# HGRN2 attention into a rational-Padé layer on one core: 1/Q written over its own denominator, four buffers for h, p1 and p2 in whole units, and a rewritten order

## The chip, the core and the metric

The kernel runs on one core of a Trainium2 chip. The core has four engines that compute, each working through its own list of instructions in order: TensorE (PE in the profile, with its weight loads as PEld), VectorE (DVE), ScalarE (ACT) and GpSimd (POOL). SyncE (SP) issues loads and stores; GpSimd issues those that convert a type or add into their destination. All transfers share 16 DMA engines. An engine waits for another by semaphores, and everything behind a waiting instruction on its engine waits too.

The metric is device microseconds (us) for the whole program, lower is better. The kernel before was measured at 213.81, 214.25 and 214.86 us (median 214.25).

## The reference

```python
# attention: B=4, H=8, S=768, D=48
f = 1.0 / (1.0 + np.exp(-f_logit))
for t in range(S):
    state = f[:, :, t, :, None] * state + np.einsum('bhd,bhe->bhde', k[:, :, t], v[:, :, t])
    y[:, :, t] = np.einsum('bhd,bhde->bhe', q[:, :, t], state)
x = y.transpose(0, 2, 1, 3).reshape(B * S, H * D)          # 3072 x 384
# rational layer: w_in 384 x 2048, w_out 2048 x 384
h = x @ w_in
P = a[0] + a[1] * h + a[2] * h**2 + a[3] * h**3
Q = 1.0 + abs(b[0]) * abs(h) + abs(b[1]) * h**2
out = (P / (Q + 1e-06)) @ w_out
```

## The kernel before

The 3072 tokens are cut into 12 **units** of 256 tokens of one batch (unit n is chunk n // 4 of batch n % 4). A unit passes through attention and then through the rational layer. The layer's 2048 features are 16 column blocks of 128; a step on blocks 0 to 8 or 8 to 16 works on one half of the unit (128 x 2048 numbers in bf16), a step on 0 to 16 on both at once (128 x 4096).

The work is not scheduled by a compiler. The string `ORDER` (lines 19 to 99) is a hand-kept list of about 800 steps, and each engine executes its instructions in the order in which the list records them. A step is written `name unit arguments`. `@k` gives the step one of four PSUM slots, which it gets when the last reader of the slot's earlier contents is done. `!mK` names an instruction, and `^mK` on another makes that one wait until the named one is done (`behind`, line 578); this is how GpSimd's work is held back. The steps, with the engine that runs them:

- `ld` loads f, k, q (SP) or v (GpSimd, with a cast to bf16); `wi` and `wo` load w_in and w_out (GpSimd, with a cast), in eight and four pieces.
- Attention: `ef`, `ls` (ACT) make log(1 + exp(-f)); `cs` (PE) sums it over tokens; `A` (ACT) takes exp of the sums; `xa n x` (line 330) multiplies q (x = 0) or k (x = 1) by it, whole (128 x 768) or in halves (128 x 384), on DVE, or on GpSimd where the step ends in `p`; `T` (PE) transposes, `Te` copies it out of PSUM; `sc`, `mk` are the masked scores (PE, DVE); `ic`, `si`, `st` advance the state (PE, PE, DVE); `vm` copies columns of v; `yi`, `yb` (PE) and `ye` (ACT or DVE) make x.
- Rational layer: `h` (PE, line 472) multiplies by w_in, four blocks into one slot; `hy` (ACT, line 487) copies them to SBUF as bf16. `sq` (DVE) or `sa` (ACT) squares into h2; `ab` (DVE) writes |h| into z; `zv` (DVE) or `zd` (an adding DMA that GpSimd issues) adds h2 to z; `rq` (ACT, line 513) takes 1/Q of z. `p1` (DVE, line 524) writes a3 h + a2 into g; `pm` (DVE) multiplies g by h2; `p2` (DVE, line 529) writes a1 h + a0 over h; `tv` (DVE) or `ta` (adding DMA) adds that to g; `gm` (DVE, line 546) multiplies g by 1/Q. `o` (PE, line 550) multiplies by w_out, `oe` copies out and `so` stores.

The arrays of the layer live in rings of buffers: unit n uses buffer n mod the ring's size (line 172):

```python
for key, n in (("hy", 3), ("h2", 2), ("z", 2), ("g", 3), ("qi", 2)):
    rings(key, n, [KF, NT], BF16)
```

So `hy` of unit n may begin once the last reader of h of unit n - 3 (its `ta` or `tv`) is done, `ab` of unit n once `rq` of unit n - 2 is, `rq` of unit n once `gm` of unit n - 2 is, and `p1` of unit n once `o` of unit n - 3 is.

ScalarE needs one table for exp and log and another for 1/Q; `tab` switches them.

Of the kernel before, what the change touches and what calls it, by code (L numbers as in the profile page):

```python
# [8 lines left out]
F32 = mybir.dt.float32  # L9
# [15 lines left out]
xa 1 0 0 2; Te 0 2 4 s; xa 1 0 2 4; ef 2; si 0 1; sc 0 1 @0; xa 1 1 0 2; st 0 1; T 1 @1; mk 0 0; ld 2 k
mk 0 1 !m5; yb 0 0 2 @3; yi 0 1; Te 1; ef 3; yb 0 2 4; ic 1 @2; ls 2; st 1 0 !m1; sc 1 1 @0; ld 2 v ^m1
ye 0 s; cs 2 @1; mk 1 1 !m3; ls 3; sc 1 0 @3; wi 0 0 8; A 2 0; si 1 1; ld 5 f; cs 3 @0; wi 3 0 8; st 1 1
A 2 1; vm 1 v !m4; wi 2 0 8; mk 1 0; xa 2 0 0 2 p ^m0; A 3 0; h 0 8 12 @2; wi 1 0 8; xa 2 0 2 4; h 0 12 16 @1
hy 0 8 12; cz 4; fb; ld 4 f; yb 1 0 2 @3; hy 0 12 16; yb 1 2 4; xa 2 1; yi 1 1; ye 1 s; p1 0 8 16; T 2 @2
# [12 lines left out]
st 5 0; yb 4 0 2; tv 0 0 8 !m8; si 5 1; hy 2 0 4; h 3 4 8 @0; ld 6 q; ld 6 v ^m8; st 5 1; gm 0 0 8; yi 4 1
# [65 lines left out]
def kernel(  # L108
# [63 lines left out]
    for key, n in (("hy", 3), ("h2", 2), ("z", 2), ("g", 3), ("qi", 2)):  # L172
        rings(key, n, [KF, NT], BF16)
# [71 lines left out]
    def const_z(i):  # L245
# [383 lines left out]
```

## Time and profile before

| | us |
|---|---|
| median of three runs | 214.25 |
| the profiled execution: its time | 213.87 |
| its span from first to last instruction | 212.2 |
| PE busy in it | 190.1 |
| DVE busy in it | 190.8 |
| ACT busy in it | 186.7 |
| POOL busy in it | 81.5 |

The profile is of one execution. The clock that TensorE was granted was 0.994 of full speed over the span. A row of a group of instructions reads: line, engine, operation, out<-in, shapes, xcount, then busy time, mean ns of one and the idle time of the engine before them. A row of a timeline reads: start, duration, engine, line, operation, and in brackets the idle time before it with what ended it. Instructions of one engine that follow each other without a wait overlap a little in these records (the next one starts before the one ahead is recorded as ended), so the time from start to start is somewhat shorter than the duration.

### The profile page before, as it was taken

The numbers are of one execution on the slowest core, as the hardware profiler recorded it, in microseconds if no ns is written. First come the engines' busy times: TensorE is split into PE (matmuls) and PEld (weight loads), VectorE is DVE, ScalarE is ACT, GpSimd is POOL, SyncE is SP. The second block draws the span as 40 slices with busy tenths as digits, with TensorE's granted clock in tenths as the row PEclk, the third lists the DMA queues.
The fourth block names the chain that finished last, engine by engine and source line by source line (L and its number), as shares of the span: only waits on it lengthen the run. The fifth ranks groups of instructions, "written<-read, shape, count | busy, mean of one in ns | idle before, by whom it ended". The sixth has DMA issues, their size and how long they took to land.

```text
span 212.2 us, 6607 instructions
## 1 busy us (share of the span) xinstructions
PE 190.1 (90%) x2894; PEld 138.7 (65%) x2894; DVE 190.8 (90%) x236; ACT 186.7 (88%) x172; POOL 81.5 (38%) x99
## 2 busy tenths in 40 slices
PE   1296799997789999999999899999999999999991
PEld 1165587875568678766888567678766766775650
DVE  3269689999999999999999979999999999999970
ACT  4755689999887999999999699999999999999861
POOL 6050612329943438016351750551583433402000
PEclk9999999999999999999999999999999999999997
DMA  5999998999999189999999999799899999998955
GB/s 93 276 251 208 249 223 229 246 259 199 180 204 209 37 153 153 228 283 279 206 232 253 245 199 219 163 195 205 171 195 162 211 206 195 198 197 167 235 152 170
DMA packets 61820, 43.15 MB, mean 203 GB/s; under 512 B 51424, under 2 KB 56544, under 8 KB 61792
## 3 DMA queue, kind: packets, MB, share of 16 engines
q0 software_dynamic: 20528, 23.86, 68.4%
q1 hardware_dynamic: 41184, 18.78, 34.2%
q8 instruction: 22, 0.36, 0.6%
q10 hardware_dynamic: 80, 0.10, 0.2%
q14 instruction: 6, 0.05, 0.1%
HBM read 25.17 MB, written 4.72 MB: 141 GB/s over the span
## 4 chain that ended last, share of the span: by engine, by line
PE 60%; DVE 15%; DMA 12%; ACT 5%; issue 3%; POOL 3%; SPq 2%; POOLq 0%; ACTq 0%; DVEq 0%
PE op L557 28%; PE hp L477 19%; DMA w_in_sb<-in_moe_w_in_dram 5%; PE y L391 4%; DMA g<-hy 4%; DVE scm L378 3%; DMA k<-in_k_dram 3%; PE tp L347 3%; DVE qkp L333 2%; DVE g L536 2%; PE sc L370 2%; PE cs L306 2%; DVE h L493 2%; ACT qi L516 2%; DVE state L461 1%
## 5 line engine op out<-in xcount | busy, mean ns | idle before, releaser
L477 PE MATMUL hp<-x,w_in_sb 128*128 128x256 bf16 x576 | 68.0, 273 | 1.1 <-DVE state L461 0.9
L557 PE MATMUL op<-w_out_sb,g 128*128 128x384 bf16 x384 | 68.6, 326 | 0.0
L477 PEld LDWEIGHTS <-w_in_sb 128*128 128x128 bf16 x576 | 55.5, 98 | 10.4 <-issue 1.9
L489 ACT CAST hy<-hp 128x1024 bf16<-128x1024 f32 x48 | 47.8, 1027 | 5.0 <-PE hp L477 3.1
L557 PEld LDWEIGHTS <-g 128*128 128x128 bf16 x384 | 35.8, 98 | 23.8 <-issue 1.2
L516 ACT ACTIVATE qi<-z 128x4096 bf16<-128x4096 bf16 (+1 forms) x16 | 44.4, 2777 | 1.1 <-DVE z L507 1.1
L511 POOL DMA_DIRECT2D z<-h x20 | 21.5, 1120 | 26.1 <-ACT h L498 18.1
L378 DVE TENSOR_TENSOR scm<-sc,mask 128x1024 bf16<-128x1024 f32 x24 | 28.8, 1214 | 1.5 <-PE sc L370 1.4
L548 DVE TENSOR_TENSOR g<-g,qi 128x2048 bf16<-128x2048 bf16 (+2 forms) x24 | 28.9, 1217 | 0.9 <-ACT qi L516 0.7
L536 DVE TENSOR_TENSOR g<-g,h 128x2048 bf16<-128x2048 bf16 (+1 forms) x21 | 29.4, 1401 | 0.1
L498 ACT ACTIVATE h<-hy 128x2048 bf16<-128x2048 bf16 (+1 forms) x13 | 26.8, 2072 | 0.0
L540 POOL DMA_DIRECT2D g<-hy x15 | 13.8, 938 | 28.1 <-DVE g L536 10.4
L328 ACT ACTIVATE A<-cs 128x768 f32<-128x768 f32 (+3 forms) x26 | 19.0, 779 | 4.5 <-PE cs L314 4.5
L333 POOL TENSOR_TENSOR qkp<-k,A 128x384 bf16<-128x384 f32 x11 | 13.0, 1218 | 23.4 <-DVE g L548 10.6
L306 PE MATMUL cs<-lsp,Ui 128*128 128x384 bf16 (+1 forms) x39 | 11.1, 345 | 10.4 <-ACT lsp L296 10.4
L526 DVE TENSOR_SCALAR g<-hy,a_sb 128x2048 bf16<-128x2048 bf16 (+1 forms) x23 | 19.0, 832 | 0.6 <-ACT hy L489 0.6
L209 POOL DMA_DIRECT2D v<-in_v_dram x12 | 12.4, 1037 | 17.6 <-DVE state L461 8.8
L531 DVE TENSOR_SCALAR hy<-hy,a_sb 128x2048 bf16<-128x2048 bf16 (+1 forms) x20 | 18.6, 928 | 0.4
L333 POOL TENSOR_TENSOR qkp<-q,A 128x384 bf16<-128x384 f32 x10 | 12.6, 1268 | 9.9 <-ACT A L328 5.3
L502 DVE TENSOR_SCALAR z<-hy 128x2048 uint16<-128x2048 uint16 (+1 forms) x21 | 15.7, 759 | 0.0
L347 PE MATMUL tp<-ident,qkp 128*128 128x128 bf16 x192 | 13.7, 227 | 2.0 <-DVE qkp L333 1.4
L391 PE MATMUL y<-scm,v 64*32 64x128 bf16 x384 | 14.0, 218 | 0.8 <-DVE scm L378 0.7
(71 smaller groups left out, 245.0 us busy)
## 6 DMA issues: line engine op xcount, KB each, us to landing
z<-h POOLq DMA_DIRECT2D x20, 512.0 KB, 7.2
g<-hy POOLq DMA_DIRECT2D x15, 512.0 KB, 7.5
f<-in_f_logit_dram SPq DMA_DIRECT2D x11, 384.0 KB, 6.9
k<-in_k_dram SPq DMA_DIRECT2D x11, 384.0 KB, 8.2
q<-in_q_dram SPq DMA_DIRECT2D x11, 384.0 KB, 7.5
v<-in_v_dram POOLq DMA_DIRECT2D x12, 192.0 KB, 7.3
out_dram<-f SPq DMA_DIRECT2D x12, 192.0 KB, 3.6
out_dram<-osb SPq DMA_DIRECT2D x10, 192.0 KB, 5.0
```

The lines of the kernel that those rows point to most:

```text
L333: i = (nc.gpsimd if eng == "p" else nc.vector).tensor_mul(s["qk"][:, x, :, hh, 0:D], s["qk"[x]][:, hh].rearrange("p h i d -> p i h d"), s[ ...
L347: nc.tensor.transpose(t[:, x, i, p, :], s["qk"][:, x, i, 2 * p:2 * p + 2, :].rearrange("t h d -> t (h d)"), ident)
L378: return nc.vector.tensor_mul(t, s["sc", g].rearrange("s r a i t -> s (r a) (i t)"), mb)
L391: nc.tensor.matmul(s["y"][32 * a:32 * a + 32, j, kk * C:kk * C + C].rearrange("e (i t) -> e i t", i=2), lhsT, rhs, start=(j, a) not in s[" ...
L477: nc.tensor.matmul(t[:, m - m0, :].rearrange("f (j t) -> f j t", j=UB), w_in_sb[:, kk, m * P:(m + 1) * P], s["x"][:, :, kk, :], start=(kk ...
L489: nc.scalar.copy(fl(big(s, "hy"), m0, m1), fl(s["hp", m0], 0, m1 - m0))
L498: return nc.scalar.activation(fl(big(s, "h2"), m0, m1), fl(big(s, "hy"), m0, m1), AF.Square)
L511: return nc.gpsimd.dma_start(out=fl(big(s, "z"), m0, m1), in_=fl(big(s, "h2"), m0, m1), accum_op=ALU.add)
L516: return nc.scalar.add_instruction(mybir.InstActivation(name=nc.get_next_instruction_name(), func=AF.Reciprocal, ins=[nc.scalar.lower_ap(f ...
L536: return nc.vector.tensor_mul(fl(big(s, "g"), m0, m1), fl(big(s, "g"), m0, m1), fl(big(s, "h2"), m0, m1))
L548: return nc.vector.tensor_mul(fl(big(s, "g"), m0, m1), fl(big(s, "g"), m0, m1), fl(big(s, "qi"), m0, m1))
L557: nc.tensor.matmul(s["op", g][:, j, 0:DM], big(s, "g")[:, m, C * j:C * j + C], w_out_sb[:, m, :], start=(s["on", j] == 1), stop=(s["on", j ...
```

## The change

The ring `qi` is gone, and `rq` writes 1/Q over z, from where `gm` reads it. z has three buffers in place of two, and hy four in place of three, so that the space stays what it was. A step that nothing used (`dm`) and the memset of its zeros (`cz 4`) are gone. The list of steps is rewritten throughout; two of its lines stand here for all.

```diff
-cu 1; cz 1; ld 0 f 2 4; ld 0 v; ab_ b s; cz 3; cz 0; ld 0 f 0 2; ci; ld 0 q 2 4; ld 1 f; cu 0; ld 0 k 0 2
-ef 0 2 4; ls 0 2 4; cm; ld 0 k 2 4; cz 2; fa; cs 0 2 4 @0; ef 0 0 2; ls 0 0 2; ld 0 q 0 2; cs 0 0 2 @1; ld 1 k
+ci; ld 0 f 0 2; cu 1; ld 0 f 2 4; ld 0 q 0 2; ld 0 v; ab_ b s; ld 1 f; cu 0; ld 0 k 0 2; ef 0 0 2; ls 0 0 2
+cm; ef 0 2 4; cz 1; ld 0 k 2 4; ls 0 2 4; cz 0; ld 0 q 2 4; cz 2; cz 3; cs 0 2 4 @0; cs 0 0 2 @1; ld 1 q
...
-    for key, n in (("hy", 3), ("h2", 2), ("z", 2), ("g", 3), ("qi", 2)):
+    for key, n in (("hy", 4), ("h2", 2), ("z", 3), ("g", 3)):
         rings(key, n, [KF, NT], BF16)
...
-        elif i == 4:
-            return nc.vector.memset(zz, 0.0)
...
             outs=[nc.scalar.lower_ap(fl(big(s, "qi"), m0, m1))]))
+            outs=[nc.scalar.lower_ap(fl(big(s, "z"), m0, m1))]))
...
-        return nc.vector.tensor_mul(fl(big(s, "g"), m0, m1), fl(big(s, "g"), m0, m1), fl(big(s, "qi"), m0, m1))
+        return nc.vector.tensor_mul(fl(big(s, "g"), m0, m1), fl(big(s, "g"), m0, m1), fl(big(s, "z"), m0, m1))
```

Counted over the two lists, the steps whose number or width differs are these:

| step | before | after |
|---|---|---|
| p1 on both halves / on one | 1 / 22 | 5 / 14 |
| p2 on both halves / on one | 4 / 16 | 5 / 14 |
| ab on both halves / on one | 3 / 18 | 0 / 24 |
| rq on both halves / on one | 8 / 8 | 6 / 12 |
| xa on DVE, whole / in halves | 4 / 19 | 2 / 24 |
| xa on GpSimd | 21 | 20 |
| Te on DVE, oe on DVE | 1, 0 | 2, 1 |

The xa that leaves GpSimd is that of q of unit 2, heads 0 to 3. Te of the first half of unit 0 goes from ACT to DVE, as does one of the last two oe.

Three places of the lists follow, engine by engine. A number right behind a name is the buffer of the ring (hy1 is buffer 1 of hy), the number behind the underscore is the build's own.

**First place: ScalarE around the copies of h of unit 7.** Before, unit 7 is in hy1 (and unit 6 in hy0), and 1/Q of unit 3 is written to qi1:

```order
L516 ACTIVATE qi1_117<-z1_112 128x2048
L454 ACTIVATE x3_137<-y_2227 128x768
L489 CAST hy0_106<-hp_2213 128x1024
L489 CAST hy0_106<-hp_2321 128x1024
L489 CAST hy0_106<-hp_2197 128x1024
L516 ACTIVATE qi1_117<-z1_112 128x2048
L489 CAST hy1_107<-hp_2354 128x1024
L357 COPY T0_132<-tp_2371 128x1024
L489 CAST hy1_107<-hp_2339 128x1024
L516 ACTIVATE qi0_116<-z0_111 128x4096
```

After, unit 7 is in hy3:

```order
L508 ACTIVATE z0_111<-z0_111 128x2048
L452 ACTIVATE x3_136<-y_2193 128x768
L481 CAST hy2_107<-hp_2241 128x1024
L481 CAST hy2_107<-hp_2319 128x1024
L481 CAST hy3_108<-hp_2335 128x1024
L508 ACTIVATE z0_111<-z0_111 128x2048
L355 COPY T0_131<-tp_2350 128x1024
L481 CAST hy2_107<-hp_2302 128x1024
L481 CAST hy3_108<-hp_2370 128x1024
L508 ACTIVATE z1_112<-z1_112 128x4096
```

One copy of unit 7 has moved ahead of the second 1/Q, the other behind Te of unit 8; hy1 was last used by unit 4, hy3 by unit 3.

**Second place: GpSimd and VectorE around the loads of w_out.** The COPY is vm, the TENSOR_TENSOR are xa. GpSimd before:

```order
L333 TENSOR_TENSOR qkp0_80<-q1_125,A0_130 128x2x4x48
L511 DMA z0_111<-h20_109 128x2048
L333 TENSOR_TENSOR qkp0_80<-k1_122,A0_130 128x2x4x48
L385 COPY vmp1_85<-v0_127 128x8x2x16
L209 DMA v2_129<-in_v_dram 128x8x96
L221 DMA w_out_sb_105<-in_moe_w_out_dram 128x4x384 x3
L333 TENSOR_TENSOR qkp1_81<-k2_123,A1_131 128x2x4x48 x2
L385 COPY vmp0_84<-v1_128 128x8x2x16
L221 DMA w_out_sb_105<-in_moe_w_out_dram 128x4x384
L333 TENSOR_TENSOR qkp1_81<-q2_126,A1_131 128x2x4x48 x2
```

GpSimd after:

```order
L331 TENSOR_TENSOR qkp0_79<-q1_124,A0_129 128x2x4x48
L503 DMA z0_111<-h20_109 128x2048
L383 COPY vmp1_84<-v0_126 128x8x2x16
L331 TENSOR_TENSOR qkp0_79<-k1_121,A0_129 128x2x4x48
L209 DMA v2_128<-in_v_dram 128x8x96
L221 DMA w_out_sb_104<-in_moe_w_out_dram 128x4x384 x2
L331 TENSOR_TENSOR qkp1_80<-k2_122,A1_130 128x2x4x48 x2
L383 COPY vmp0_83<-v1_127 128x8x2x16
L221 DMA w_out_sb_104<-in_moe_w_out_dram 128x4x384
L331 TENSOR_TENSOR qkp1_80<-q2_125,A1_130 128x2x4x48 x2
L221 DMA w_out_sb_104<-in_moe_w_out_dram 128x4x384
```

VectorE in the same stretch, before:

```order
L378 TENSOR_TENSOR scm0_133<-sc_944,mask_76 128x1024
L461 TENSOR_TENSOR state3_1_96<-sv_981,A1_131 128x384
L493 TENSOR_TENSOR h20_109<-hy0_106 128x2048
L536 TENSOR_TENSOR g0_113<-g0_113,h20_109 128x2048
L461 TENSOR_TENSOR state3_2_97<-sv_981,A1_131 128x384
L378 TENSOR_TENSOR scm0_133<-sc_1035,mask_76 128x1024
L333 TENSOR_TENSOR qkp0_80<-k1_122,A0_130 128x2x4x48
L333 TENSOR_TENSOR qkp0_80<-q1_125,A0_130 128x2x4x48
L526 TENSOR_SCALAR g1_114<-hy1_107,a_sb_98 128x2048
L536 TENSOR_TENSOR g1_114<-g1_114,h21_110 128x2048
```

and after:

```order
L376 TENSOR_TENSOR scm0_132<-sc_959,mask_76 128x1024
L331 TENSOR_TENSOR qkp0_79<-q1_124,A0_129 128x2x4x48
L485 TENSOR_TENSOR h20_109<-hy0_105 128x2048
L528 TENSOR_TENSOR g0_114<-g0_114,h20_109 128x2048
L459 TENSOR_TENSOR state3_2_96<-sv_941,A1_130 128x384
L376 TENSOR_TENSOR scm0_132<-sc_1031,mask_76 128x1024
L331 TENSOR_TENSOR qkp0_79<-k1_121,A0_129 128x2x4x48
L518 TENSOR_SCALAR g1_115<-hy1_106,a_sb_97 128x2048
L528 TENSOR_TENSOR g1_115<-g1_115,h21_110 128x2048
```

VectorE's q product of unit 4 has moved ahead of the square of unit 0, the other stays behind the scores of unit 3; one of GpSimd's four loads of w_out has moved behind its products of unit 5.

**Third place: VectorE from gm of unit 1 to p1 of unit 4.** Before, p1 of units 3 and 4 (L526) are half steps:

```order
L548 TENSOR_TENSOR g1_114<-g1_114,qi1_117 128x2048 x2
L502 TENSOR_SCALAR z1_112<-hy0_106 128x2048 x2
L493 TENSOR_TENSOR h20_109<-hy1_107 128x2048
L526 TENSOR_SCALAR g0_113<-hy0_106,a_sb_98 128x2048
L548 TENSOR_TENSOR g2_115<-g2_115,qi0_116 128x2048
L536 TENSOR_TENSOR g0_113<-g0_113,h21_110 128x2048
L548 TENSOR_TENSOR g2_115<-g2_115,qi0_116 128x2048
L378 TENSOR_TENSOR scm0_133<-sc_1873,mask_76 128x1024
L378 TENSOR_TENSOR scm0_133<-sc_1855,mask_76 128x1024
L526 TENSOR_SCALAR g1_114<-hy1_107,a_sb_98 128x2048
```

After:

```order
L540 TENSOR_TENSOR g1_115<-g1_115,z1_112 128x2048 x2
L485 TENSOR_TENSOR h20_109<-hy0_105 128x2048
L494 TENSOR_SCALAR z1_112<-hy0_105 128x2048
L518 TENSOR_SCALAR g0_114<-hy3_108,a_sb_97 128x4096
L540 TENSOR_TENSOR g2_116<-g2_116,z2_113 128x4096
L518 TENSOR_SCALAR g1_115<-hy0_105,a_sb_97 128x4096
L376 TENSOR_TENSOR scm0_132<-sc_1843,mask_76 128x1024
```

p1 of unit 4 (into g1, which unit 1 used) is one step of 4096 now, and stands ahead of the scores of unit 6 instead of behind them.

More of the change, by code (lines that the diff above doesn't have):

```diff
@@ L25 @@
[L25 to L29, printed above, removed]
@@ L464, in st @@
             _at(s["ae"], [[DM + 16 if n else DM // 2 + 8, 2], [1, 4], [0, D]], 4 * j))
-    def dm(i, sl):
-        t = slot(sl, [P, 2, 512], F32, "dm")
-        for b in range(2):
-            nc.tensor.matmul(t[:, b, :], zz[:, 0:P], zz, start=True, stop=True)
     def h(n, m0, m1, sl):
```

154 lines of the change are left out of this document (79 added, 75 removed).

## The prediction

> **What bounds the kernel now.** I read the page's busy shares first, then the same by stretches of 10 us, then the chain of waits. Columns of the second view: the stretch, its length, busy time and instructions of each engine, granted clock, DMA share, GB/s.
>
> ```profile
> PE 190.1 (90%) x2894; PEld 138.7 (65%) x2894; DVE 190.8 (90%) x236; ACT 186.7 (88%) x172; POOL 81.5 (38%) x99
> ...
> 0.00:10.00 10.00, 1.87 (x20) 1.77 (x21) 3.20 (x25) 5.82 (x10) 3.26 (x13) 1.00 0.90 176
> 20.00:30.00 10.00, 8.46 (x223) 6.75 (x216) 7.68 (x13) 6.51 (x8) 4.13 (x6) 1.00 1.24 234
> 40.00:50.00 10.00, 8.97 (x197) 6.96 (x192) 9.96 (x13) 9.85 (x12) 3.39 (x4) 1.00 1.29 249
> 50.00:60.00 10.00, 7.42 (x196) 5.40 (x195) 9.90 (x11) 8.52 (x8) 9.99 (x12) 1.00 1.20 179
> 110.00:120.00 10.00, 10.00 (x167) 7.99 (x166) 10.00 (x12) 8.80 (x8) 4.19 (x6) 1.00 1.08 245
> 120.00:130.00 10.00, 8.59 (x181) 5.85 (x180) 8.56 (x9) 9.49 (x8) 4.07 (x5) 1.00 1.30 219
> ```
>
> Three engines are full at once from about 30 us on: no stretch can become shorter by taking work from one alone. TensorE's instructions are the same in both lists, so its time is its work plus the holes in it, and holes are left in few places: up to 30 us, where the loads come in; 1.03 us at 40 to 50; 2.58 at 50 to 60; 1.41 at 120 to 130. In 50 to 60 VectorE has no hole (9.90) while TensorE has: there VectorE is the bound, and what it does in those 10 us counts in full. At 120 to 130 both have holes, 1.41 and 1.44, and ScalarE has one just before. That hole is on the chain of waits (start, duration, what):
>
> ```profile
> 111.76 8.62 DMA g<-hy
> ...
> 121.39 1.02 ACT T L357
> ...
> 129.71 1.05 PE tp L347 x16
> ```
>
> and in the timelines of ScalarE and VectorE:
>
> ```profile
> 120.48 1.01 ACT L489 CAST hy<-hp 128x1024 bf16<-128x1024 f32 x1 [1.65 <-DMA g<-hy]
> ...
> 123.57 2.36 DVE L378 TENSOR_TENSOR scm<-sc,mask 128x1024 bf16<-128x1024 f32 x2 [0.95 <-PE sc L370]
> 126.87 2.29 DVE L548 TENSOR_TENSOR g<-g,qi 128x4096 bf16<-128x4096 bf16 x1 [0.49 <-ACT qi L516]
> ```
>
> The copy of h of unit 7 goes over h of unit 4, and the adding DMA that still reads unit 4 lands at 120.4. ScalarE stands for 1.65 us, Te of unit 8 is late behind it, then the scores, then VectorE's mask and gm of unit 4.
>
> **The change, part by part.** The sum is made against the profiled execution, 213.87 us; the median of the runs is 0.38 above it.
>
> Four buffers for hy. Unit 7 now follows unit 3, whose adds were done long before. The wait of 1.65 us goes, and with it VectorE's 0.95 + 0.49 = 1.44 us and TensorE's 1.41. What is late next there is gm itself, costed below. I take -1.4; the bounds are 0 (another wait takes the place at once) and -1.65.
>
> z in place of qi. ab of unit n had to wait for 1/Q of unit n - 2 on another engine; now it follows gm of unit n - 3 on its own engine, which needs no wait. It reads and writes the same count as before. 0.
>
> Wider p1 and p2. The rows for the two widths (busy us, mean ns):
>
> ```profile
> L526 DVE TENSOR_SCALAR g<-hy,a_sb 128x2048 bf16<-128x2048 bf16 x22 | 17.6, 808 | 0.6 <-ACT hy L489 0.6
> L526 DVE TENSOR_SCALAR g<-hy,a_sb 128x4096 bf16<-128x4096 bf16 x1 | 1.3, 1343 | 0.0
> L531 DVE TENSOR_SCALAR hy<-hy,a_sb 128x2048 bf16<-128x2048 bf16 x16 | 13.2, 824 | 0.3
> L531 DVE TENSOR_SCALAR hy<-hy,a_sb 128x4096 bf16<-128x4096 bf16 x4 | 5.4, 1340 | 0.1
> L502 DVE TENSOR_SCALAR z<-hy 128x2048 uint16<-128x2048 uint16 x18 | 12.0, 683 | 0.0
> L502 DVE TENSOR_SCALAR z<-hy 128x4096 uint16<-128x4096 uint16 x3 | 3.7, 1217 | 0.0
> L333 DVE TENSOR_TENSOR qkp<-q,A 128x384 bf16<-128x384 f32 x12 | 7.7, 645 | 1.0 <-DMA q<-in_q_dram 1.0
> L333 DVE TENSOR_TENSOR qkp<-k,A 128x768 bf16<-128x768 f32 x3 | 2.8, 946 | 0.0
> ```
>
> Two halves of p1 cost 2 x 808 - 1343 = 273 ns more than one whole, less about 80 ns by which neighbours overlap (gm of unit 1 below: 2 x 1.22 recorded as 2.36): 0.19 us. Ten whole steps sounds like much, but five stood there already; five joins more, four of p1 and one of p2 at some 0.2, make -1.0. Against them: three abs are split, each 2 x 683 - 1217 - 80 = 70 ns, +0.2; two whole products are split, 2 x 645 - 946 - 80 = 0.26 each, +0.5; a half product comes from GpSimd, +0.5; the unused memset goes, -0.3 by its place before the first product of k of unit 2. VectorE's work is thus the same, -0.1. ScalarE gets two 1/Q in halves more (under 0.2) and gives up one copy early on: 0.
>
> GpSimd's products. VectorE is slowed at some places where GpSimd works (timeline of VectorE, then of GpSimd; the last VectorE row is an undisturbed product):
>
> ```profile
> 36.41 2.02 DVE L544 TENSOR_TENSOR g<-g,hy 128x2048 bf16<-128x2048 bf16 x1
> ...
> 50.60 1.38 DVE L333 TENSOR_TENSOR qkp<-k,A 128x384 bf16<-128x384 f32 x1
> 51.91 1.35 DVE L333 TENSOR_TENSOR qkp<-q,A 128x384 bf16<-128x384 f32 x1
> ...
> 54.16 1.83 DVE L536 TENSOR_TENSOR g<-g,h 128x2048 bf16<-128x2048 bf16 x1
> ...
> 58.44 1.06 DVE L531 TENSOR_SCALAR hy<-hy,a_sb 128x2048 bf16<-128x2048 bf16 x1
> ...
> 61.66 1.21 DVE L544 TENSOR_TENSOR g<-g,hy 128x2048 bf16<-128x2048 bf16 x1
> ...
> 97.90 0.55 DVE L333 TENSOR_TENSOR qkp<-q,A 128x384 bf16<-128x384 f32 x1
> ```
>
> ```profile
> 36.00 1.35 POOL L333 TENSOR_TENSOR qkp<-q,A 128x384 bf16<-128x384 f32 x1 [1.64 <-ACT lsp L296]
> ...
> 51.16 2.38 POOL L221 DMA_DIRECT2D w_out_sb<-in_moe_w_out_dram  x3
> 53.42 3.42 POOL L333 TENSOR_TENSOR qkp<-k,A 128x384 bf16<-128x384 f32 x2
> ...
> 57.93 2.42 POOL L333 TENSOR_TENSOR qkp<-q,A 128x384 bf16<-128x384 f32 x2
> ```
>
> The excess over an undisturbed one is 0.81 for the add at 36.41, 0.83 and 0.80 for the two products, about 0.6 for pm at 54.16, 0.25 for p2 at 58.44. In the new lists the product of q of unit 4 stands behind the scores of unit 3, before GpSimd may begin the issue that waits for the square of unit 0: 0.80 saved. The other product stays beside the loads of v and w_out, and pm still meets GpSimd's products of unit 5, which come one issue earlier while pm comes one product earlier: nothing saved. p2 is now past before GpSimd's q products: 0.25. The add of unit 0 meets the product of unit 3 later, since GpSimd issues a load of v first: I take half, 0.4. Behind 62 us VectorE shows no such excess. Sum -1.4; bounds 0, and -3.3 if all five go. All of it lies where VectorE is the bound and TensorE has 2.58 us of holes.
>
> [...]
>
> The start. The four loads of w_in that the first h needs are issued behind a load of v, which waits for the last product of unit 0; the chain has them as
>
> ```profile
> 13.87 1.66 POOL w_in_sb L215 x3
> 15.54 9.76 DMA w_in_sb<-in_moe_w_in_dram
> ...
> 25.43 2.79 PE hp L477 x24
> ```
>
> In the new list one product of q of unit 0 comes before the load of k that all four waited for, one product of 0.5 us less behind it. The loads share the DMA engines with others (DMA share 1.24 at 20 to 30), so an earlier issue need not land as much earlier: I take -0.3, of 0 to -0.5.
>
> New waits. gm of unit 3 follows the add that it needs more closely: from pm's end to gm VectorE now has vm, an ab, a p1, two half products, two squares and an add on 2048, and two masks, 8.2 us by the rows of these kinds, and that DMA takes
>
> ```profile
> g<-hy POOLq DMA_DIRECT2D x15, 512.0 KB, 7.5
> ```
>
> in the median, 8.62 in the chain above. That and its like cost 0 to 2; I take +0.5 us, nearer to the bottom since most leads are as long as before.
>
> Sum: -1.4 - 0.1 - 1.4 - 0.3 + 0.5 = -2.7, so 211.2 for a profiled execution and, 0.38 higher, **211.5 us** as a median. TensorE has the room: its holes from 40 us on are 1.03 + 2.58 + 1.41 = 5.0.
>
> **The rivals.** A: the products aren't held where it matters. Several of them wait for marks long past (those of unit 5 for ab and tv of unit 0), so the queue decides. Then VectorE's five slow steps stay or change places, the hole at 120 goes, and new waits cost 1.0, half their bound: 213.87 - 1.4 - 0.1 - 0.3 + 1.0 + 0.38 = 213.5. For it: the order of GpSimd's rows is hardly changed there. Against: VectorE's q product did move.
>
> B, slower: the joined p1 holds VectorE for TensorE. g has three buffers still, so p1 of unit 4 over both halves needs the last o of unit 1:
>
> ```profile
> 85.56 2.36 DVE L548 TENSOR_TENSOR g<-g,qi 128x2048 bf16<-128x2048 bf16 x2
> ...
> 89.05 1.22 DVE L493 TENSOR_TENSOR h<-hy 128x2048 bf16<-128x2048 bf16 x1
> ...
> 96.58 0.80 DVE L526 TENSOR_SCALAR g<-hy,a_sb 128x2048 bf16<-128x2048 bf16 x1
> ```
>
> ```profile
> 87.40 6.01 PE L557 MATMUL op<-w_out_sb,g 128*128 128x384 bf16 x36
> ```
>
> 32 of the 36 are unit 1's, at 6.01 / 36 = 0.167 us done at 92.7, 6.0 us after the first of these gm ended (half of 2.36 behind 85.56, so 86.7). In the new list VectorE reaches p1 of unit 4 after the second gm, a square, an abs, a whole p1 and a whole gm, each by its row less the 0.08 of overlap: 1.14 + 1.14 + 0.6 + 1.26 + 2.2 = 6.3. It has 0.3 us to spare, where the first half before started at 96.6, 4 us after TensorE was done, and the second later still. The same holds for p1 of units 3, 6 and 10. If TensorE runs 1.5 us further behind than here, each of the four waits 1.2 and everything behind it on VectorE too: +4.8, 216.3 us. It decides from 0.3 us of lag on. Against it: TensorE's lag in this profile is that of the list before, and it gains as much from the closed holes as VectorE.
>
> C: all five slow steps go and nothing new waits: -1.4 - 0.1 - 3.3 - 0.5 = 208.6 + 0.38 = 209.0.
>
> **How the numbers follow.** My forecast 0.56, A 0.19, B 0.20, C 0.05. A difference of under 0.5%, 1.07 us, can't be told from none; the bounds are 213.2 and 215.3. Faster by more: 0.54 of the forecast, 0.05 of A and C's 0.05, 0.64. Slower by more: B, 0.20. Within: 0.16. The forecast's own range is 209.5 to 213.2; with A, and B up to its middle, 208.8 to 215.8 leaves out some 2 in 10.
>
> **What would show it.** In the changed profile ScalarE's copies of h wait for no adding DMA, and the stretch that holds gm of unit 4 has TensorE and VectorE at 9.9 or more. Of the products on VectorE before 60 us one at most takes over 1 us. p1 rows of 4096 count five, at 1.3 us, with no idle time before them put down to TensorE's o; if they have it, B was right. First h at 25.1 or a little earlier. The prediction is wrong if TensorE has more than 3 us of holes between 40 and 200 us, or if VectorE's holes there are over 2.5.

## The result, and the profile after

| | before | after |
|---|---|---|
| median of 20 runs each, us | 213.92 | 216.01 |
| the profiled execution, us | 213.87 | 215.81 |
| its span, us | 212.2 | 214.1 |
| mean clock granted to TensorE over it | 0.994 | 0.980 |

The ratio of after to before is 1.0109, 95% interval 1.0076 to 1.0142: the change is slower by 1.1%, some 2.3 us. The forecast was 2.7 us faster. The medians in this text are of all runs; the ratios leave out runs that took over 1.5% more than the fastest of their kernel, so a ratio is not the quotient of two medians.

The page's busy line and its row of TensorE's clock (tenths of full speed in 40 slices of 5.35 us), for the changed kernel:

```profile
PE 193.9 (91%) x2894; PEld 140.0 (65%) x2894; DVE 192.1 (90%) x238; ACT 185.4 (87%) x172; POOL 81.6 (38%) x98
...
PEclk9999889999988999999999999999999999999998
```

Before, the row of the clock reads

```profile
PEclk9999999999999999999999999999999999999997
```

TensorE has the same 2894 matmuls and is busy 3.8 us longer (190.1 before); its clock was halved for two stretches of 3.41 us, which by themselves make 3.4 of it. By stretches (columns as in the prediction: stretch, length, PE, PEld, DVE, ACT, POOL, clock, DMA share, GB/s):

```profile
20.00:30.00 10.00, 7.94 (x134) 5.50 (x127) 7.40 (x13) 4.07 (x5) 3.15 (x5) 0.83 1.22 226
50.00:60.00 10.00, 8.05 (x240) 6.04 (x237) 9.89 (x11) 9.78 (x9) 9.97 (x12) 1.00 1.12 178
60.00:70.00 10.00, 9.07 (x116) 6.82 (x116) 9.92 (x13) 6.92 (x8) 4.74 (x5) 0.83 1.24 208
120.00:130.00 10.00, 9.11 (x178) 5.72 (x177) 10.00 (x11) 9.97 (x8) 7.29 (x8) 1.00 1.28 165
```

The hole of VectorE at 120 to 130 is closed (8.56 before, 10.00 now); TensorE's is not quite (8.59, now 9.11). The time is lost ahead of that, as the same steps in the two profiled executions show (start in us):

| step | before | after | late by |
|---|---|---|---|
| first mask of unit 0 (VectorE) | 17.47 | 17.46 | 0.0 |
| A of unit 2 (ScalarE) | 23.78 | 26.41 | 2.6 |
| first copy of h (ScalarE) | 26.94 | 28.79 | 1.9 |
| state of unit 5 (VectorE) | 61.19 | 61.57 | 0.4 |
| second mask of unit 6 (VectorE) | 95.45 | 97.23 | 1.8 |
| 1/Q of unit 4 (ScalarE) | 123.20 | 123.87 | 0.7 |
| second mask of unit 10 (VectorE) | 155.74 | 157.83 | 2.1 |
| first product with 1/Q of unit 11 (VectorE) | 201.69 | 202.98 | 1.3 |

Most of it is regained at 50 to 60 us, lost again behind that, regained at 120 and lost again. A table of two single executions can't say what each part is worth: the first copy of h came between 25.55 and 29.18 us in the nine profiles with the start of before (that of before and eight of kernels below), and between 28.46 and 29.59 in the three with the new one. The experiments cut the list instead.

VectorE at the start of the changed kernel (timeline; the small rows are `fa`, the nine steps on b, the first and the last of them shown):

```profile
9.41 0.23 DVE L383 COPY vmp<-v 128x256 bf16<-128x256 bf16 x1 [2.98 <-DMA v<-in_v_dram]
9.55 0.55 DVE L331 TENSOR_TENSOR qkp<-q,A 128x384 bf16<-128x384 f32 x1
10.02 0.16 DVE L262 TENSOR_SCALAR bm<-b_sb 128x2 uint32<-128x2 uint32 x1
...
11.36 0.16 DVE L270 SCALAR_TENSOR_TENSOR sig<-bm,sig 128x1 f32<-128x1 f32 x1
11.44 1.03 DVE L331 TENSOR_TENSOR qkp<-k,A 128x384 bf16<-128x384 f32 x2
12.38 0.55 DVE L331 TENSOR_TENSOR qkp<-q,A 128x384 bf16<-128x384 f32 x1
```

The copy of v stands ahead of the first product and waits 2.98 us for its load; `fa` stands behind that product and takes 1.42 us. The last product of unit 0 ends at 12.93, not earlier than before (12.65) but later.

VectorE, then GpSimd, at the places where they meet:

```profile
47.72 0.54 DVE L331 TENSOR_TENSOR qkp<-q,A 128x384 bf16<-128x384 f32 x1
...
52.17 0.55 DVE L331 TENSOR_TENSOR qkp<-k,A 128x384 bf16<-128x384 f32 x1
...
53.55 2.00 DVE L528 TENSOR_TENSOR g<-g,h 128x2048 bf16<-128x2048 bf16 x1
...
58.00 2.05 DVE L523 TENSOR_SCALAR hy<-hy,a_sb 128x2048 bf16<-128x2048 bf16 x1
...
75.04 1.32 DVE L331 TENSOR_TENSOR qkp<-k,A 128x384 bf16<-128x384 f32 x1
...
123.32 1.01 DVE L494 TENSOR_SCALAR z<-hy 128x2048 uint16<-128x2048 uint16 x1
```

```profile
52.77 1.71 POOL L221 DMA_DIRECT2D w_out_sb<-in_moe_w_out_dram  x2
54.49 2.87 POOL L331 TENSOR_TENSOR qkp<-k,A 128x384 bf16<-128x384 f32 x2
...
57.66 0.79 POOL L221 DMA_DIRECT2D w_out_sb<-in_moe_w_out_dram  x1
58.47 2.43 POOL L331 TENSOR_TENSOR qkp<-q,A 128x384 bf16<-128x384 f32 x2
...
74.94 1.00 POOL L331 TENSOR_TENSOR qkp<-k,A 128x384 bf16<-128x384 f32 x1 [10.21 <-ACT A L326]
...
122.19 1.62 POOL L209 DMA_DIRECT2D v<-in_v_dram  x1
```

Both products of unit 4 now take 0.55 (1.38 and 1.35 before). In their place p2 of unit 0 takes 2.05 (1.06 before, 0.80 undisturbed), pm of unit 1 2.00 (1.83 before, 1.22 undisturbed), a product of unit 6 1.32 and an abs 1.01 in place of 0.68. Six steps before and six now take over 0.15 us more than the median of their shape, 3.7 us in all before and 3.8 now: the slow steps changed places.

### The profile page after: what moved, and what is told of

Read it like the earlier page. It is cut to its first block, busy times and chain, and to the rows that moved or that the text cites. A ratio compares the mean times of both kernels' runs of the same rounds, so it can differ in the third digit from the quotient of the medians.

```text
span 214.1 us, 6608 instructions
## 1 busy us (share of the span) xinstructions
PE 193.9 (91%) x2894; PEld 140.0 (65%) x2894; DVE 192.1 (90%) x238; ACT 185.4 (87%) x172; POOL 81.6 (38%) x98
## 5 line engine op out<-in xcount | busy, mean ns | idle before, releaser
L469 PE MATMUL hp<-x,w_in_sb 128*128 128x256 bf16 x576 | 70.1, 278 | 0.0
L469 PEld LDWEIGHTS <-w_in_sb 128*128 128x128 bf16 x576 | 56.3, 100 | 9.8 <-issue 0.8
L508 ACT ACTIVATE z<-z 128x2048 bf16<-128x2048 bf16 (+1 forms) x18 | 45.0, 2504 | 0.0
L540 DVE TENSOR_TENSOR g<-g,z 128x2048 bf16<-128x2048 bf16 (+2 forms) x24 | 29.1, 1226 | 0.6 <-ACT z L508 0.5
L532 POOL DMA_DIRECT2D g<-hy x15 | 17.5, 1187 | 30.7 <-DVE g L528 8.7
L523 DVE TENSOR_SCALAR hy<-hy,a_sb 128x2048 bf16<-128x2048 bf16 (+1 forms) x19 | 19.2, 1012 | 0.4
L209 POOL DMA_DIRECT2D v<-in_v_dram x12 | 13.1, 1090 | 16.7 <-DVE qkp L331 9.0
L518 DVE TENSOR_SCALAR g<-hy,a_sb 128x2048 bf16<-128x2048 bf16 (+1 forms) x19 | 17.9, 947 | 0.1
L494 DVE TENSOR_SCALAR z<-hy 128x2048 uint16<-128x2048 uint16 x24 | 16.8, 703 | 0.0
L459 DVE TENSOR_TENSOR state<-sv,A 128x384 bf16<-128x384 f32 x20 | 10.9, 550 | 3.6 <-PE sv L444 2.0
```

The lines of the kernel that those rows point to most:

```text
L469: nc.tensor.matmul(t[:, m - m0, :].rearrange("f (j t) -> f j t", j=UB), w_in_sb[:, kk, m * P:(m + 1) * P], s["x"][:, :, kk, :], start=(kk ...
L508: return nc.scalar.add_instruction(mybir.InstActivation(name=nc.get_next_instruction_name(), func=AF.Reciprocal, ins=[nc.scalar.lower_ap(f ...
L518: return nc.vector.tensor_scalar(fl(big(s, "g"), m0, m1), fl(big(s, "hy"), m0, m1), a_sb[:, 3:4], a_sb[:, 2:3], op0=ALU.mult, op1=ALU.add)
L523: return nc.vector.tensor_scalar(fl(big(s, "hy"), m0, m1), fl(big(s, "hy"), m0, m1), a_sb[:, 1:2], a_sb[:, 0:1], op0=ALU.mult, op1=ALU.add)
L540: return nc.vector.tensor_mul(fl(big(s, "g"), m0, m1), fl(big(s, "g"), m0, m1), fl(big(s, "z"), m0, m1))
```

## The experiments

Ratios are to the kernel before, run on the same chip alongside, with their 95% intervals.

### Where the time is lost: the two lists cut and joined

At two places the lists have come through almost the same steps: ahead of the first rational step (28 us) and behind the first product with 1/Q (61 us). There one list can be carried on with the other. The first kernel is before's list with the new buffers alone:

```diff
-    for key, n in (("hy", 3), ("h2", 2), ("z", 2), ("g", 3), ("qi", 2)):
+    for key, n in (("hy", 4), ("h2", 2), ("z", 3), ("g", 3)):
```

with 1/Q written over z as in the change.

> The order of before, with the buffers of the change (four of hy, three of z, 1/Q written over z). Theory of the prediction: the hole at 120 us closes by itself and is worth -1.4 us, so 212.5 us, a ratio of 0.993, with no adding DMA ahead of a copy of h. Rival: something else stands at the same place at once (1/Q of unit 4, the adds), and the ratio is 1.000 within 0.003. A second rival: 1/Q over z holds ScalarE or VectorE somewhere, ratio over 1.003.

> The change with the steps up to the first p1 (about 30 us) in the order of before; from there on, and in its buffers, the change as it is. If the start costs the 1.9 us by which the first copy of h is later in the change's profile, the ratio to before falls from 1.011 to 1.002 (214.4 us). If a late start is caught up later anyway (VectorE's steps at 56 to 61 us are only 0.4 us late), it stays at 1.008 to 1.011. If the dips of TensorE's clock come from the idle of the start, this run shows one window of half clock fewer.

> The change with everything up to 1/Q's product of unit 0 (about 61 us) in the order of before, the rest and the buffers as in the change. Theory that GpSimd's products only changed places, with p2 of unit 0 (2.05 us) as the price: about the same as with the old start alone, within 0.5 us. Theory that the middle gained what was forecast (0.80 for the product of q of unit 4, 0.4 for the add): 1.2 us slower than with the old start alone. Theory that everything lost lies before 61 us: 212.5 us, a ratio of 0.993, since the hole at 120 us is closed.

| start | to 61 us | rest | buffers | median, us | ratio |
|---|---|---|---|---|---|
| old | old | old | new | 212.27 | 0.9885 [0.9848, 0.9922] |
| old | old | new | new | 215.00 | 1.0010 [0.9969, 1.0052] |
| old | new | new | new | 213.67 | 0.9990 [0.9945, 1.0034] |
| new | new | new | new | 216.01 | 1.0109 [1.0076, 1.0142] |

Read from row to row: the buffers alone gain 1.15%, 2.5 us. The new order behind 61 us gives all of it back, 1.25% or 2.7 us. The new middle is worth nothing that can be told (0.2%). The new start costs 1.2%, 2.5 us. Each step is uncertain by some 0.6% (the root of the two half intervals squared and added); the quotients of the medians of all runs give -0.8, +1.3, -0.6 and +1.2% for the four. The theory that everything lost lies before 61 us falls with the second row, and with the third the hope that a halved window goes with the old start: that kernel's profile still has two.

What the buffers do where they were meant to work is seen on VectorE in the first of these kernels:

```profile
122.36 0.68 DVE L502 TENSOR_SCALAR z<-hy 128x2048 uint16<-128x2048 uint16 x1
122.97 2.34 DVE L378 TENSOR_TENSOR scm<-sc,mask 128x1024 bf16<-128x1024 f32 x2
...
126.90 2.29 DVE L548 TENSOR_TENSOR g<-g,z 128x4096 bf16<-128x4096 bf16 x1 [1.13 <-issue]
```

The masks follow without the 0.95 us of before. But VectorE then stands 1.13 us ahead of the product with 1/Q of unit 4, more than the 0.49 of before, so that at this place its idle time falls from 1.44 to 1.13 us only. The 1/Q is done at 125.50; what is late is the adding DMA of unit 4, by the records landed at 126.82. The chain of waits has it:

```profile
117.44 8.33 DMA g<-hy
```

From 62 us to the end this profile gains 1.2 us on before's, 0.4 of it here; where the rest of the measured 2.5 us comes from its rows don't show.

The converse, the new order with the old buffers:

> The order of the change, with the buffers of before (three of hy, two of z, two of 1/Q). If the buffers are worth 1.4 us in this order too, 217.4 us, a ratio to before of about 1.017; if the new order doesn't need them, the 1.011 of the change.

1.0465 [1.0405, 1.0525]. In this list several copies of h stand ahead of the last reads of h three units earlier (of unit 4 ahead of p2 of unit 1, of 6, 7 and 9 likewise), and abs of units 5, 7 and 9 ahead of 1/Q two units earlier, so with the old buffers h and z are overwritten too early. Its time is that of another computation and prices nothing; it shows that the order can't do without the buffers.

### The start

```diff
 cz 2; cz 3
+fa
 cs 0 2 4 @0; cs 0 0 2 @1; ld 1 q
-vm 0 v
 A 0 0 0 2; A 0 0 2 4; xa 0 0 0 2; ef 1; ld 1 k
-fa
 A 0 1 2 4; A 0 1 0 2; ls 1; xa 0 1 2 4; ld 2 f; xa 0 1 0 2
+vm 0 v
 cs 1 @2
```

> The change with two things of its first 12 us where they stood before: the nine small steps of VectorE on b ahead of the products of unit 0, and the copy of v of unit 0 behind its product of k. TensorE's order at 21 to 25 us stays as in the change. If VectorE's late products of unit 0 set the start (the last at 12.93 us, 12.06 before), the first copy of h comes about 1 us earlier and the ratio to before falls from 1.011 to about 1.005. If TensorE's order at 21 to 25 us sets it, the first copy of h stays at 28.8 and the ratio at 1.011.

1.0019 [0.9979, 1.0059], down from 1.0109. (The 12.06 of the expectation is a row of the run with the old start; in the profile of before it is 12.65.) VectorE in it:

```profile
8.15 0.56 DVE L327 TENSOR_TENSOR qkp<-q,A 128x384 bf16<-128x384 f32 x1 [0.20 <-ACT A L322]
10.40 1.03 DVE L327 TENSOR_TENSOR qkp<-k,A 128x384 bf16<-128x384 f32 x2 [1.69 <-ACT A L322]
11.35 0.22 DVE L379 COPY vmp<-v 128x256 bf16<-128x256 bf16 x1
11.48 0.55 DVE L327 TENSOR_TENSOR qkp<-q,A 128x384 bf16<-128x384 f32 x1
```

The first product comes at 8.15 and not 9.55, the last ends at 12.03 and not 12.93. The first copy of h is at 28.04 and not 28.79. These two small edits are 0.9% of the start's 1.2%, in part, it seems, by way of the clock: seven of these 12 runs have a mean clock of 0.992 or more, of the change's 20 four. What is left to the order of TensorE's steps at 21 to 25 us, 0.3%, is within the uncertainty.

### The clock, and a stop of TensorE at 20 to 22 us

The changed kernel's trace cut along the windows in which the clock was halved (the windows before and behind them too):

```profile
21.27:24.68 3.41, 1.51 (x46) 1.00 (x39) 2.63 (x4) 0.08 (x1) 2.41 (x4) 1.00 1.09 228
24.68:28.09 3.41, 3.41 (x29) 2.12 (x27) 1.71 (x7) 1.69 (x3) 0.74 (x2) 0.50 1.40 260
58.81:62.22 3.41, 1.86 (x77) 1.30 (x73) 3.41 (x5) 2.35 (x2) 3.41 (x5) 1.00 1.25 206
62.22:65.63 3.41, 3.41 (x24) 2.33 (x17) 3.41 (x5) 2.94 (x3) 2.52 (x3) 0.50 1.27 204
```

TensorE was busy 1.51 and 1.86 of 3.41 us, 44% and 55%; the next 3.41 us ran at half clock. The same count over the full-clock windows up to 200 us in the 14 traces of this study: the clock fell behind each of the 15 windows with a busy share of 0.549 or less, and behind none of 0.550 or more. The lull of before at 52.8 us had 0.555 in its profile and just escaped, and so did, with 0.550, the second lull of the kernel with the two steps of the start put back. The mark fits these lulls and isn't the whole rule: behind three windows in the last 10 us, with 0.43, 0.47 and 0.51, the clock stayed full.

The stretches of full clock in the records are whole multiples of 3.41 us (2, 10 and 43 in the change, 57 before), and the windows lie at other points of the span in the two traces: the records of full clock begin at 17.85 us in the change, at 15.26 before. That a lull may so fall into one window or be split by two is the author's reading, not tested apart. Runs of one kernel differ: the buffers alone took 210.30 to 210.62 us in the three runs with a mean clock of 0.998 or more, and 211.70 to 213.09 in seven with 0.990 to 0.992, one halved window. The change has two lulls that reach the mark: 16 of its 20 runs have a mean clock of 0.984 or less, two windows or more, and its one run at 1.000 took 213.88, no better than before's median. In the other kernels with at least two runs of each kind the means lie 0.9 to 2.2 us apart, with one exception: of the kernel with early fillers below, six runs at 0.996 or more took 211.12 to 212.60 us, and four at 0.986 to 0.992 took 210.81 to 212.92.

Part of the first lull isn't a wait for data. TensorE's rows of the changed kernel, two groups of the second unit's scores with nothing between them:

```profile
21.10 0.42 PE L368 MATMUL sc<-T 48*64 48x128 bf16 x16 [0.16 <-DVE T L356]
23.42 0.42 PE L368 MATMUL sc<-T 48*64 48x128 bf16 x16 [1.90 <-DVE scm L376]
```

and of the old order with the new buffers, where sums (`cs`) come next:

```profile
19.85 0.42 PE L370 MATMUL sc<-T 48*64 48x128 bf16 x16
22.74 0.32 PE L306 MATMUL cs<-lsp,Ui 128*128 128x384 bf16 x1 [2.47 <-issue]
```

Other work stands behind the stop, and a different releaser is named, but 223 matmuls are recorded ahead of it in both, as in all 14 traces (the expectation below counts from 0 and calls the last one the 222nd). A queue of the page's part 3 (packets, MB, share of 16 engines) moves 16 KB a packet:

```profile
q8 instruction: 22, 0.36, 0.6%
```

By the records of the packets, the first lands some 1.3 to 1.5 us ahead of the point where TensorE goes on:

| kernel | last matmul starts | packet lands | next starts | behind the packet |
|---|---|---|---|---|
| before | 21.25 | 21.38 | 22.70 | 1.32 |
| the change | 21.30 | 22.10 | 23.42 | 1.32 |
| old order, new buffers | 20.05 | 21.28 | 22.74 | 1.46 |
| old start | 19.90 | 20.53 | 21.92 | 1.39 |

A test that tells instructions from data is to add matmuls ahead of it:

```diff
 cu 1; cz 1
+cz 4
 ld 0 f 2 4
...
+dm 0 @3; dm 0 @3; dm 0 @3
 cs 0 2 4 @0; ef 0 0 2; ls 0 0 2; ld 0 q 0 2; cs 0 0 2 @1
+dm 0 @3; dm 0 @3; dm 0 @3; dm 0 @3; dm 0 @3
 ld 1 k
...
 hy 0 8 12
-cz 4
 fb
```

> The order of before with the buffers of the change (0.9885), and 16 matmuls of 512 columns of zeros into a free slot of PSUM while TensorE has nothing to do, 6 of them before the first cumulative sums and 10 behind them; nothing reads them. Theory of the clock: TensorE reaches full clock by 9 us instead of 15 to 18, the first transposes and scores are faster, and the start gains 0.5 to 1.5 us: a ratio of 0.982 to 0.986. Rival: the start is bound by loads and VectorE, and the ratio stays at 0.9885. Second theory, on the stop of TensorE at 20 to 23 us that comes behind its 222nd matmul in every trace so far: if it waits for its next 16 KB of instructions, the stop comes behind the 222nd matmul again, 16 matmuls earlier in the program (inside the second unit's scores); if it waits for data, it stays behind those scores, at the 238th.

```profile
19.37 0.51 PE L432 MATMUL sv<-v,qkp 64*128 64x96 bf16 x16
20.21 0.42 PE L366 MATMUL sc<-T 48*64 48x128 bf16 x16 [0.33 <-DVE T L354]
20.56 0.34 PE L302 MATMUL cs<-lsp,Ui 128*128 128x384 bf16 x1
```

The stop moved: 223 matmuls, the fillers among them, are again ahead of it, and it now stands ahead of the scores; the sums behind them follow at once, where TensorE stood 2.7 us without the fillers. The packet landed at 18.86 and TensorE went on at 20.21, 1.35 us behind it. This stop, 0.53 us from start to start, is weak evidence by itself, since the scores also need VectorE's copy T, which is recorded to 19.93:

```profile
18.71 1.22 DVE L354 COPY T<-tp 128x2048 bf16<-128x2048 bf16 x1
```

What speaks for the instructions is that the stop ahead of the sums is gone. Of the two sentences that were on record, that of the instructions is the one that holds. With the fillers the records of full clock begin at 5.46 us (before at 15.26, where 16 transposes take 1.89 us ahead of that and 1.07 behind), no window is halved in this profile, and the first copy of h came at 24.77, earlier than in any of the nine profiles of the old start without them (25.55 to 29.18). But the ratio was 0.9917 [0.9879, 0.9954], no better than without them: the forecast of 0.982 to 0.986 fails. The rival's ratio is the nearer one, but its reason, a start bound by loads and VectorE, isn't what this profile shows; why the runs gain nothing by the earlier start stays open.

Fillers in the lulls of the change itself (50 matmuls into unread columns of y at five places between 54 and 62 us):

> The change with 50 matmuls of 128 columns into columns of y that nothing reads, at the five places between 54 and 62 us where TensorE waits. Theory that the second window of half clock follows from TensorE's idle there: that window is gone from the records, where it stood in most runs of the change (mean clock 0.984), and the median falls by 1 to 1.4 us, a ratio to before of about 1.005. Rival: the fillers delay as much as they save, or the window has another cause: ratio 1.011.

The second halved window is gone (one is left, at 25.75 to 29.16), and the kernel is slower yet: 1.0188 [1.0141, 1.0236]. Weight loads of TensorE in it:

```profile
63.00 0.09 PEld L385 LDWEIGHTS <-v 64*32 64x32 bf16 x2
64.67 0.09 PEld L385 LDWEIGHTS <-v 64*32 64x32 bf16 x2 [1.58 <-issue]
```

By the records, 1978 weight loads and matmuls are ahead of this stop and 446 ahead of the first one. The seventh packet of instructions landed at 63.03, 1.64 us ahead of the second row. The change without the fillers doesn't show this second stop; that the fillers brought it is the author's inference. So the price of the clock was not shown by taking the windows away; it stands on the runs of one kernel that differ in them, with the exception named.

### GpSimd beside VectorE

Behind 61 us, two edits on the kernel with the old order up to there:

```diff
 pm 4 8 16
+ld 9 q
 ld 10 q; si 7 0 @1; yb 6 0 2; A 8 0
-ld 9 q
...
 zd 5 8 16
+vm 8 ^m17
 xa 9 1 0 2 p ^m17; o 3 1 12 16; st 8 0; mk 8 0 !m23; sc 8 1 @3; yi 8 1 @1; xa 9 1 2 4 p ^m18; yi 8 0; o 3 0 8 12; mk 8 1
-vm 8 ^m17
```

> The kernel with everything up to 61 us as before and the rest as in the change (1.001), with two edits behind 90 us: the load of q of unit 9 ahead of that of q of unit 10, and GpSimd's copy of v of unit 8 ahead of its products of k of unit 9. Theory of contention: the product of q of unit 9 on GpSimd then runs beside a mask and not beside the square of unit 5, which falls from 2.02 to 1.21 us; TensorE's wait for that copy at 127 us (0.8 us) goes; together -0.8 to -1.2 us, a ratio of about 0.996. Rival: the product meets another VectorE step and slows that by as much: 1.001.

```profile
109.56 1.24 DVE L481 TENSOR_TENSOR h<-hy 128x2048 bf16<-128x2048 bf16 x1
110.72 1.21 DVE L372 TENSOR_TENSOR scm<-sc,mask 128x1024 bf16<-128x1024 f32 x1
...
112.32 1.21 DVE L481 TENSOR_TENSOR h<-hy 128x2048 bf16<-128x2048 bf16 x1
```

```profile
109.64 2.00 POOL L327 TENSOR_TENSOR qkp<-q,A 128x384 bf16<-128x384 f32 x1
```

The square at 112.32 fell from 2.02 to 1.21, and now it is GpSimd's product that takes 2.00: it began 0.08 us behind the other square, which took 1.24, and ended 0.84 behind that one's end. Without the repair it had begun at 111.72, 0.37 ahead of the square, and took 1.31, and the square ended 1.08 behind its end. In both pairs the one that began second is the long one; the mask at 110.72, which reads PSUM and stands beside the rest of the product, keeps its 1.21. TensorE's wait for the copy of v of unit 8 is gone too. The profiled end is 1.2 us earlier (spans 212.0 and 213.2, clock 0.992 in both), but the ratio, 1.0002 [0.9965, 1.0038], can't be told from 1.0010.

Three repairs together, on the change with the old start: those two, and

```diff
-wo 0 4
 p2 0 0 8 !m11; yb 4 2 4
-xa 5 0 0 2 p ^m9
+xa 5 0 0 2 p ^m11
 sc 4 0 @2; st 4 1; yi 4 1; ld 6 q
-xa 5 0 2 4 p ^m10
+xa 5 0 2 4 p ^m11; wo 0 4
```

> The change with the old start (0.999) and three repairs that keep GpSimd's work away from VectorE's steps: its products of q of unit 5 held behind p2 of unit 0, with the last issue of a load of w_out behind them; the load of q of unit 9 ahead of that of unit 10; its copy of v of unit 8 ahead of its products of k of unit 9. Theory of contention: p2 of unit 0 falls from 2.04 to 0.80 us, the square of unit 5 stays at 1.21, and the sum is -2.4 us, a ratio of 0.988. Rival: GpSimd's work meets other steps instead, which take as much: 0.996 to 0.999.

0.9913 [0.9876, 0.9950], from 0.9990 without them: some 1.6 us of the 2.4, uncertain by 1.2. p2 of unit 0:

```profile
58.32 0.80 DVE L519 TENSOR_SCALAR hy<-hy,a_sb 128x2048 bf16<-128x2048 bf16 x1
59.04 0.55 DVE L455 TENSOR_TENSOR state<-sv,A 128x384 bf16<-128x384 f32 x1
59.51 1.21 DVE L372 TENSOR_TENSOR scm<-sc,mask 128x1024 bf16<-128x1024 f32 x1
```

with GpSimd's two products, held, beside the state and the mask (59.20 to 61.17, 1.97 for the two, where one takes 0.99 or 1.00 in its fastest rows). The contention was part of what the change lost; the three were run as one, so what each is worth stays open. Repaired, the new order is still not measurably faster than the old one with the new buffers.

On that one, GpSimd's issues of w_out were moved behind pm of unit 1 (`wo 12 16 ^m13; wo 8 12 ^m13; wo 4 8 ^m13`), and then also its copy of v of unit 4 ahead of them and its products of unit 5 behind p2 of unit 0:

> The order of before with the buffers of the change (0.9885), and three issues of loads of w_out by GpSimd moved from beside VectorE's products of k and q of unit 4 to behind pm of unit 1. If the issues slow those products (1.38 and 1.35 us beside them), both take 0.55, and pm of unit 1, which then meets nothing, 1.22 in place of 1.84: -2.3 us, less what the issues and GpSimd's products slow later, a ratio of about 0.982 to 0.985. If an instruction that only writes does not contend, the two products stay at 1.3 to 1.4 us.

> The order of before with the buffers of the change (0.9885), three issues of w_out behind pm of unit 1 as in the run before this one, and GpSimd's copy of v of unit 4 now ahead of them, its four products of unit 5 and the last issue behind p2 of unit 0. If the run before this one lost what it gained to TensorE's wait of 2.38 us for that copy, the wait is gone here, VectorE's products of unit 4, pm of unit 1 and p2 of unit 0 keep 0.55, 1.22 and 0.80 us, and -2.5 us remain less up to 1.6 for the steps that the four products now meet: a ratio of 0.980 to 0.985. Rival: GpSimd's work costs VectorE as much wherever it stands, and the ratio is 0.988 or more.

In both the products of unit 4 take 0.55 each and pm of unit 1 1.23 (1.38, 1.35 and 1.84 without the edit). VectorE in the first, and the issue by GpSimd that stands beside its first product:

```profile
50.47 0.55 DVE L329 TENSOR_TENSOR qkp<-k,A 128x384 bf16<-128x384 f32 x1
50.94 0.55 DVE L329 TENSOR_TENSOR qkp<-q,A 128x384 bf16<-128x384 f32 x1
...
52.32 1.23 DVE L532 TENSOR_TENSOR g<-g,h 128x2048 bf16<-128x2048 bf16 x1
```

```profile
50.10 1.05 POOL L205 DMA_DIRECT2D v<-in_v_dram  x1
```

So the issues of w_out did slow VectorE's products, and the issue of a load of v did not: it stands beside the first product here, begun 0.37 us ahead of it, as it does without the edit, where that product takes 1.38. What sets the two kinds of issue apart no run shows. The 1.3 to 1.4 us of the expectation's second case did not come. The time did not follow: 0.9957 [0.9904, 1.0009] for the first, where TensorE then waited 2.15 us for the copy of v of unit 4 and its clock was halved behind that (its mean over the span 0.992), and 0.9900 [0.9843, 0.9957] for the second, where it no longer waits for it. VectorE is 1.8 us less slowed there than with the buffers alone, though the add of unit 0 now meets a product (2.01 in place of 1.21) and a hole of 1.10 opened ahead of a state. Its last steps come 1.9 us earlier than in the profile of the buffers alone, 0.7 of which stands already at 45 us, ahead of the edit; the ratio doesn't show it. Neither measurably beats the buffers alone.

### p1 joined

On the old order with the new buffers, p1 of units 2, 3, 4, 8 and 10 in one step each, for instance

```diff
-p1 4 8 16
+p1 4 0 16
...
-p1 4 0 8
```

> The order of before with the buffers of the change (0.9885), and p1 of units 2, 3, 4, 8 and 10 joined into one step each, as the change does. By the prediction's 0.19 us each -0.95, a ratio of 0.984, with no idle ahead of these steps. By its rival B VectorE waits for TensorE's last o ahead of them, 1.2 us at each of units 3 and 4: ratio over 0.995.

0.9969 [0.9929, 1.0010]: joining gains nothing, and may cost some. The ratio lies where rival B put it, but not for its reason: no joined step has idle time ahead of it that is put down to TensorE's o. In its profile VectorE is 2.5 us ahead of the unjoined one's at 30 to 66 us (this execution had no halved window at the start, the other one), and at its last steps 1.9 ahead: the five savings of 0.19 are not found again.

## Why the prediction was wrong

Point by point, with the forecast in the order of its sum:

- **Buffers, forecast -1.4:** right that they gain, and measured larger, -2.5 us (0.9885, from -1.7 to -3.3). ScalarE's copies wait for TensorE alone, in the changed kernel too, and there VectorE's hole at 120 is closed. In the old order it isn't: most of it passed to a wait for the adding DMA of unit 4 (0.95 + 0.49 us before, 1.13 now), which is what the prediction's bound of 0 stood for, "another wait takes the place at once". Where the rest of the gain arises, and which of the two rings brings it, is not shown.
- **Wider p1 and p2, -0.1:** the rows are as forecast (five p1 of 4096 at 1.34, no idle), the effect about nil or a small cost. The 0.26 for splitting a product was misread: its 645 ns is a mean that holds slowed rows, the longest of 1.35, and an undisturbed half takes 0.55, which makes it 0.07. Rival B's wait for TensorE's last o did not come.
- **GpSimd's products, -1.4: the step that failed in the middle.** The product of q of unit 4 was gained as argued, and the other product as well. The add is not slow any more, but not by the order: in eight profiles with the old order at that place it takes 2.02 in three and 1.20 to 1.22 in five, so its 0.4 was read from one execution. And the sum took from each slow step what moving away saves and asked of none what the moved work meets next: p2, forecast to be past before GpSimd's products, lost 1.25 us to them and not 0.25; pm lost 0.78 (0.62 before), and a product of unit 6, an abs and others came on top. Rival A, slow steps that change places, was the case here, with 0.19; its 213.5 left out the start and the clock.
- **The start, -0.3: the largest miss, +2.5.** The sentence "one product of q of unit 0 comes before the load of k" counted the product that was moved and not what was moved past it on the same engine: the copy of v with its wait for a load, and `fa`. Both stand in the third line of the new list. Putting those two back gains 0.9%. The first h, forecast at 25.1 or a little earlier, came at 26.50.
- **New waits, +0.5 of 0 to 2:** the adds that were feared hold nothing up in the rows of the change that are shown, though one does in the old order with the new buffers (1.13 us). What came is TensorE's wait for the copy of v of unit 8, 0.89 us at 129 us, behind GpSimd's products, and the new order behind 61 us costs 2.7 us in all. Of that the profiles place 1.3 us in contention and some of the rest in new small waits of VectorE (0.66 ahead of a mask of unit 7, 0.5 ahead of the product with 1/Q of unit 6); how it is divided in the measured time stays open.
- **The clock was in no term.** The sum took the granted clock of one execution (0.994) as the kernel's. The change deepened two lulls, and a halved window goes with 1 to 2 us in the runs of most kernels here. The 0.38 from the profiled execution to the median was that of three runs; with 20 it is 0.05.

The marks set for being wrong were both met: from 40 to 200 us TensorE has 3.8 us of holes and VectorE 2.8, by the last row of the same view over these 16 stretches:

```profile
sum 160.00, PE 156.23 PEld 112.73 DVE 157.17 ACT 153.72 POOL 70.08; mean PE 9.76 PEld 7.05 DVE 9.82 ACT 9.61 POOL 4.38
```

Before, the same row has TensorE at 154.85 and VectorE at 157.00: of VectorE's 3.0 us of holes 0.2 were closed, so next to nothing of the forecast gain arrived there.

## What to carry to other kernels

A change that bundles new buffers with a rewritten order should be measured apart: here the buffers alone are 1.15% faster than before (the lowest ratio of all kernels run here, though three others lie within its uncertainty), and the order takes it back twice. Where a step is moved to the front, list everything on that engine that now stands between it and the work that is waited for, small set-up steps and waits for loads included. Where a slow step is freed from a contending engine, ask at once which step the moved work meets next: here p2 of unit 0 took 2.05 us beside GpSimd's products, and the masks, which read PSUM, kept their 1.21.

## What was not expected of the hardware

- TensorE stood in every trace with 446 or 447 weight loads and matmuls recorded ahead, at 20 to 22 us, and went on 1.3 to 1.5 us after the first packet of 16 KB on the instruction queue had landed; 0.5 to 2.7 us pass between the starts on both sides of the stop. That it waits for its instructions is the author's reading of the run with early fillers, where the stop kept its 223 matmuls ahead and left its place ahead of the sums. TensorE stood again 1532 further on in the change with fillers (1.67 us) and with the three repairs (0.52). The DMA share beside the first stop of the change was 1.09 (the row of 21.27 above).
- The clock fell to half behind windows of 3.41 us in which TensorE was busy for under 55%, in 15 of 15 up to 200 us, though behind none of three such windows in the last 10 us. It came back after one window of 3.41 us, but for two cases (the three repairs, and the new order with the old buffers) in which it took two.
- Three issues of loads of w_out by GpSimd slowed products on VectorE with two inputs in SBUF from 0.55 to 1.38 and 1.35 us; the issue of a load of v beside such a product left it at 0.55. An issue can be slow itself: one of a load of v took 1.62 us beside the slowed abs of the change, where two took 1.88 at 113 us.
